# A second weight left whole in float32 for batch 0, with a new table of order, in a three-stage attention and mixture kernel on one core

## The chip, the core and the metric

The kernel runs on one core of one Trainium2 chip. The core has a matrix engine (PE in the profile; its weight loads are the row PEld), a vector engine (DVE), a scalar engine (ACT), a general engine (POOL) and a queue that issues transfers (SP). The metric is the device time of one execution in microseconds (us), lower is better.

## The reference

Three stages follow one another on a batch of 4 sequences of 576 tokens with 512 features.

```python
# 1 windowed attention, 8 heads of 64: four plain (window 32), four dilated by 4
attn = softmax(where(mask, q @ k.T / 8, -1e9)) @ v
# 2 gated mixture
xk = mu_k * x + (1 - mu_k) * x_prev ; xr = mu_r * x + (1 - mu_r) * x_prev
k  = relu(xk @ w_k) ; v = (k * k) @ w_v ; r = sigmoid(xr @ w_r)
x  = r * v
# 3 gated unit with a spatial product
u, v = split(relu(x @ w_in)) ; v_n = normalise(v)
out  = (u * (w_spatial @ v_n + b_spatial)) @ w_out
```

w_k and w_in are 512x1024, w_v is 1024x512, w_r and w_out are 512x512. All inputs arrive as 64-bit words; one 128x512 piece of a weight is 512 KB on its way in.

## The kernel before

**Precision.** A float32 product is made of three reduced-precision products (float32r): both operands are split into a high and a low part (`halves` for activations, `split` for weights), and high·high, high·low and low·high are summed. In the trace such a product is a triple, for the weight w_r `xh,wr`, `xl,wr`, `xh,wr`. A weight named in `WHOLE` is treated otherwise in batch 0: `product` is called with `whole_`, and one real float32 matmul (two records in the trace) takes the unsplit number and the unsplit activation. Such a weight is split only after batch 0, by `split_whole`, before batch 1 needs it. Before, only "wk" stands in `WHOLE`.

**A weight's way in.** `split_weight` cuts a weight into 128x512 chunks (8 of wk, 4 of wr, 8 of wv). For each, SP loads 512 KB of words into one of four half rooms (the tiles `room`, numbers 81 and 82). ACT takes the high word into a number tile and scales the low word in place, DVE joins the two with a SCALAR_TENSOR_TENSOR that reads `room`; I call it the joining. Only then is the half room free for the load four chunks later. The number tile is one of four `temps`, or, for a whole weight, a tile of its own (`wk_..._2`). Without `WHOLE` the split follows: a CAST for the high part (ACT or DVE), a subtraction for the low part (POOL or DVE).

**Batch 0.** Its tokens are computed in two parts, 256 and 320 wide; later batches in two halves of 288. wv's split chunks lie where batch 0's attention inputs (`early`) were, so they are written after the last reader of `early`. The product with wv needs all eight chunks of wv: an output of 128x256 is 24 matmuls, three for each chunk.

**Order.** A planner (`Plan`) holds every step with a cost for each engine that may do it, a priority, and its dependencies. It simulates the engines and from that fixes the order of instructions on each engine and, where two or three engines may do a step, which does it. `TUNE` shifts the priorities and the choice of engine. In gaps that it foresees on PE in the first 100 us the planner puts matmuls on constants (`const-bfloat16-1.0`) that compute nothing; I call them fillers. `keep_warm` in `att` puts more of them between the scores of batch 0. The Tile framework adds waits and buffers, so the fixed order is what the chip executes.

**Names.** `nat_turn` turns batch 0's q and k with PE transposes, `together` puts scores of both head groups into one step. `psM`, `psS`, `psT`, `psB` are PSUM banks, `kr` and `sq_dt.float32r` hold relu and square, `ld` and `vw` are loads of later q, k and v. Nearly every instruction is recorded at one line of a helper (L499 before, L500 after).

Of the kernel before, what the change touches and what calls it, by code (L numbers as in the profile page):

```python
# [37 lines left out]
def blocks(dil):  # L38
# [14 lines left out]
WHOLE = ("wk",)  # L53
# [24 lines left out]
    ('nat', 0, 0): {'nat': (-822, -93004, 792, 22)},  # L78
    ('nat', 0, 1): {'nat': (8004, -315342, 792, 22)},
    ('nat', 1, 0): {'nat': (82855, -4474, 792, 22)},  # L80
    ('nat', 1, 1): {'nat': (-35255, 93970, 792, 22)},
    ('nat', 2, 0): {'nat': (-40032, -157092, 792, 22)},
    ('out', 0): {'egh': (25273, -268581, 0, -800), 'egl': (43089, -174119, 792, 0), 'psB': (-4330, 117521, 792, 22), 'ot': (-59436, 43359, -200, 800), 'out': (49470, 139244, 792, 22)},
    ('out', 1): {'egh': (-167582, 160854, 0, 2000), 'egl': (53746, 288389, 1500, 800), 'psB': (-134988, -179435, 792, 22), 'ot': (-56627, 219801, -200, -300), 'out': (16484, -315151, 792, 22)},
    ('out', 2): {'egh': (17548, -207273, 200, 22), 'egl': (107706, 139205, 792, 300), 'psB': (-159311, 193150, 792, 22), 'ot': (-28034, -383613, -600, -300), 'out': (-205845, -31242, 792, 22)},
    ('out', 3): {'egh': (-158193, -49852, 200, 2000), 'egl': (-111996, -51605, 400, -800), 'psB': (115712, 235954, 792, 22), 'ot': (11988, -24299, 200, 22), 'out': (15709, 251770, 792, 22)},
# [18 lines left out]
    ('sc', 0, 1, 1): {'psM': (-28310, -110097, 792, 22), 'psS': (-63150, -50215, 792, 22)},  # L105
# [17 lines left out]
    ('start',): {'ident': (-6484, -23532, 792, 22), 'identb': (-15068, 269113, 792, 22), 'xok': (48253, 184201, 792, 22), 'mask': (807, 217415, 400, 2000)},  # L123
# [387 lines left out]
def kernel(  # L511
# [61 lines left out]
    ident = get("cp", [P, P], F32, "ident")  # L573
# [1468 lines left out]
```

## Time and profile before

| | |
|---|---|
| Median of 3 runs | 577.19 us (576.16 to 577.32) |
| The profiled execution | 578.83 us, its span 577.1 us |
| Busy: PE, PEld, DVE, ACT, POOL | 97%, 87%, 61%, 44%, 16% of the span |
| Granted TensorE clock | 1.00 in the profiled execution, in nearly every stretch of 10 us |

The span runs from the first to the last instruction; the profiled execution's own time has some 1.7 us around it. Fillers count as busy time of PE, so 97% says less than it seems for the first 84 us.

### The profile page before, as it was taken

Reading aid. Unit: us, or ns where it says so; the run is one execution under the profiler, and the core shown is the slowest. Engines: PE = TensorE matmul, PEld = TensorE weight load, DVE = VectorE, ACT = ScalarE, POOL = GpSimd, SP = SyncE. Lnnn points to the kernel's source line nnn. Section 1 sums busy time; section 2 is a strip of 40 time slices with the busy share of each in tenths; the row PEclk is TensorE's granted clock in tenths of the full one; section 3 lists DMA queues with packets and bytes.
Section 4 is the critical chain, followed back from the end, with each engine's and each line's share of the span. In section 5 each row is a group of like instructions: output and inputs, shape, how many; then the busy total and the mean of one; then the engine's idle time right before and its main releaser. Section 6 shows DMA issues by size and latency. Waiting matters only on the chain.

```text
span 577.1 us, 13816 instructions
## 1 busy us (share of the span) xinstructions
PE 558.9 (97%) x5800; PEld 503.8 (87%) x5813; DVE 354.2 (61%) x784; ACT 252.7 (44%) x579; POOL 92.5 (16%) x115
## 2 busy tenths in 40 slices
PE   8889889999999999999999999999999999999997
PEld 4557677899899999999999999989889989998996
DVE  1699876987988785444975332489456337733540
ACT  1689845423545633713877242386113114311412
POOL 1111023300633402111001010013301210000040
PEclk9999999999999999999999999999999999999999
DMA  9958985356552150311340010231010020001002
GB/s 185 260 160 257 210 133 89 64 102 123 93 89 38 56 123 1 94 37 37 109 132 22 1 26 0 64 104 36 19 37 0 20 92 0 1 1 73 1 1 91
DMA packets 96253, 43.08 MB, mean 75 GB/s; under 512 B 81536, under 2 KB 89216, under 8 KB 96192
## 3 DMA queue, kind: packets, MB, share of 16 engines
q1 hardware_dynamic: 96192, 42.21, 31.4%
q8 instruction: 45, 0.74, 0.5%
q14 instruction: 16, 0.13, 0.1%
HBM read 37.47 MB, written 4.72 MB: 73 GB/s over the span
## 4 chain that ended last, share of the span: by engine, by line
PE 79%; DVE 10%; DMA 5%; ACT 3%; issue 2%; SPq 1%; DVEq 0%; ACTq 0%
PE psM L499 56%; PE psB L499 16%; PE psT L499 4%; DMA room<-in_moe_w_v_dram 3%; PE psS L499 2%; DVE xm L499 1%; DVE st L499 1%; DVE pr L499 1%; DMA room<-in_moe_w_r_dram 1%; DVE kr L499 1%; DMA early<-in_k_dram 1%; DVE wk L499 1%; DMA ld<-in_k_dram 1%; DVE xh L499 1%; SPq L499 1%
## 5 line engine op out<-in xcount | busy, mean ns | idle before, releaser
L499 PE MATMUL psM<-xh,wk 128*128 128x288 f32 (+2 forms) x512 | 124.2, 329 | 2.5 <-DVE xh L499 1.1
L499 PE MATMUL psM<-sq_dt.float32r,wv 128*128 128x288 f32 (+2 forms) x768 | 113.4, 298 | 2.3 <-ACT x L499 1.3
L499 PEld LDWEIGHTS psM<-sq_dt.float32r,wv 128*128 128x128 f32 x768 | 104.8, 188 | 5.0 <-ACT x L499 2.7
L499 PEld LDWEIGHTS psM<-xh,wk 128*128 128x128 f32 x512 | 87.6, 188 | 11.4 <-DVE xh L499 2.2
L499 PE MATMUL psM<-xh,wr 128*128 128x288 f32 (+2 forms) x256 | 63.0, 306 | 2.3 <-ACT xh L499 0.9
L499 PE MATMUL psM<-xl,wk 128*128 128x288 f32 x192 | 56.5, 294 | 0.0
L499 PE MATMUL psM<-x2h,wi 128*128 128x288 f32 x256 | 56.1, 297 | 0.0
L499 ACT ACTIVATE kr<-psM 128x288 f32<-128x288 f32 (+2 forms) x51 | 21.0, 411 | 67.8 <-PE psM L499 64.5
L499 PEld LDWEIGHTS psM<-xh,wr 128*128 128x128 f32 x256 | 44.4, 188 | 4.3 <-ACT xh L499 1.1
L499 POOL TENSOR_TENSOR xl<-xm,xh 128x288 fp32r<-128x288 f32 (+1 forms) x30 | 26.6, 896 | 130.4 <-ACT xh L499 74.9
L499 PEld LDWEIGHTS psM<-x2h,wi 128*128 128x128 f32 x256 | 42.7, 188 | 1.2 <-ACT u L499 0.7
L499 PE MATMUL psB<-wi,x2h 128*128 128x512 f32 x128 | 40.3, 396 | 0.0
L499 PE MATMUL psB<-wo,gh 128*128 128x512 f32 (+1 forms) x136 | 40.2, 379 | 0.0
L499 PE MATMUL psM<-x2l,wi 128*128 128x288 f32 x128 | 37.9, 296 | 0.9 <-DVE x2l L499 0.9
L499 PE MATMUL psM<-wsh,vl 128*128 128x288 f32 x128 | 37.9, 296 | 0.2 <-DVE vl L499 0.2
L499 PE MATMUL psM<-xl,wr 128*128 128x288 f32 (+2 forms) x128 | 37.9, 296 | 0.2
L499 PE MATMUL psM<-wsh,vh 128*128 128x288 f32 x128 | 37.9, 296 | 0.0
L499 PE MATMUL psM<-wsl,vh 128*128 128x288 f32 x128 | 37.7, 294 | 0.0
L499 PEld LDWEIGHTS psM<-xl,wk 128*128 128x128 f32 x192 | 36.1, 188 | 0.0
L499 DVE SCALAR_TENSOR_TENSOR xm<-x,mu,xm 128x288 f32<-128x288 f32 (+2 forms) x56 | 31.3, 564 | 5.8 <-ACT xm L499 5.4
L499 DVE SCALAR_TENSOR_TENSOR x<-x,psM 128x288 f32<-128x288 f32 (+2 forms) x32 | 14.4, 453 | 32.8 <-PE psM L499 25.7
L499 DVE TENSOR_TENSOR g<-psM,bb 128x288 f32<-128x288 f32 x32 | 14.3, 453 | 31.2 <-PE psM L499 27.8
(161 smaller groups left out, 1097.1 us busy)
## 6 DMA issues: line engine op xcount, KB each, us to landing
vw<-in_v_dram SPq DMA_DIRECT2D x36, 128.0 KB, 3.1
room<-in_moe_w_k_dram SPq DMA_DIRECT2D x8, 512.0 KB, 7.4
room<-in_moe_w_v_dram SPq DMA_DIRECT2D x8, 512.0 KB, 6.3
raw<-in_moe_w_in_dram SPq DMA_DIRECT2D x8, 512.0 KB, 3.8
ld<-in_q_dram SPq DMA_DIRECT2D x48, 72.0 KB, 2.6
ld<-in_k_dram SPq DMA_DIRECT2D x48, 72.0 KB, 2.7
vw<-in_v_dram SPq DMA_DIRECT2D x8, 288.0 KB, 5.6
room<-in_moe_w_r_dram SPq DMA_DIRECT2D x4, 512.0 KB, 4.8
```

What stands on the lines that cost most here:

```text
L499: return self.tc.keep_in_program_order(getattr(self.engine, name)(*args, **kw))
```

## The change

"wr" joins `WHOLE`; batch 0 multiplies w_r as one float32 matmul per term and does not split the activations for it; w_r is split after batch 0. The costs by which the planner places `nat_turn` and `together` change, and all entries of `TUNE` are new, found for the mean of replays with disturbed durations. Two of its lines stand for the table.

```diff
-WHOLE = ("wk",)
+WHOLE = ("wk", "wr")
...
-    ('w', 'wr'): {'tmp': (-19737, -299053, 792, 22), 'low': (-26769, 116870, 792, 22), 'part0': (-18161, 187096, 200, 300), 'part1': (-37782, 29061, -200, -300)},
+    ('w', 'wr'): {'whole': (-146522, -222248, 792, 22), 'low': (247288, 121722, 792, 22)},
...
+    ('w2', 'wr'): {'part0': (51813, 179976, -200, -800), 'part1': (185010, 430438, 1500, -300)},
...
-            cost, ins = 0.43 * w, 4 * len(its)
+            cost, ins = 0.94 * w, 4 * len(its)
...
-            cost, ins = len(its) * (30 + 0.4 * n), 2 * len(its)
+            cost, ins = len(its) * (70 + 0.41 * n), 2 * len(its)
...
+        steps = max(x[2] for x in infos)
...
-            for i in range(max(x[2] for x in infos)):
+            for i in range(steps):
...
-            {"pe": max(x[2] for x in infos) * (157 if b else 200 + 40 * len(infos)) + 150 * (b > 0) + sum(x[5] for x in infos)}, emit,
+            {"pe": steps * (157 if b else 94 + 63 * len(infos)) + (150 if b else 320 * -(-steps // 3)) + sum(x[5] for x in infos)}, emit,
```

Three places show how the order moves. On PE, at the start of batch 0's first product with w_r (256 wide), stood before, with `wr_0_0` a high and `wr_0_1` a low part:

```order
L499 MATMUL psM_100<-xh_0_579,wr_0_0_753 128x256
L499 MATMUL psM_100<-xl_585,wr_0_0_753 128x256
L499 MATMUL psM_100<-xh_0_579,wr_0_1_760 128x256
L499 LDWEIGHTS const-bfloat16-1.0
L499 MATMUL psT_119<-const-bfloat16-1.0 128x512
L499 MATMUL psM_100<-xh_0_582,wr_0_0_793 128x256
L499 MATMUL psM_100<-xl_587,wr_0_0_793 128x256
L499 MATMUL psM_100<-xh_0_582,wr_0_1_802 128x256
```

and after the change, `wr_0_2` being the whole number:

```order
L500 MATMUL psM_100<-xh_0_426,wr_0_2_677 128x256
L500 LDWEIGHTS const-bfloat16-1.0
L500 MATMUL psT_119<-const-bfloat16-1.0 128x512
L500 MATMUL psM_100<-xh_0_484,wr_0_2_692 128x256
L500 MATMUL psM_100<-xh_0_424,wr_0_2_726 128x256
L500 MATMUL psM_100<-xh_0_486,wr_0_2_762 128x256
```

Three matmuls became one at 32 places (16 of them 256 wide, 16 of them 320 wide). In the whole program the fillers go from 83 to 68.

On DVE, from the joining of wr's second chunk to that of its third, stood before:

```order
L499 SCALAR_TENSOR_TENSOR temps<-temps,room_82 128x512
L499 CAST sq_dt.float32r<-kr_746 128x256
L499 CAST wr_0_0_793<-temps 128x512
L499 TENSOR_TENSOR sq_dt.float32r<-kr_746,sq_dt.float32r 128x256
L499 SCALAR_TENSOR_TENSOR temps<-temps,room_81 128x512
```

and after:

```order
L500 SCALAR_TENSOR_TENSOR wr_0_2_692<-wr_0_2_692,room_82 128x512
L500 TENSOR_SCALAR st_105<-st_105 128x6
L500 RECIPROCAL st_105<-st_105 128x6
L500 CAST wr_0_0_731<-wr_0_2_692 128x512
L500 TENSOR_TENSOR pr_104<-pr_104,st_105 128x384
L500 TENSOR_TENSOR sq_dt.float32r<-kr_628,sq_dt.float32r 128x256
L500 SCALAR_TENSOR_TENSOR wr_0_2_726<-wr_0_2_726,room_81 128x512
```

The early casts of wr stay on DVE; wr's four subtractions, which stood here on DVE and POOL, are on POOL and behind the last subtraction of wk. Softmax steps of batch 0's last attention chunk (`pr_104`) moved down to this place.

On SP, around the loads of wv's last four chunks, stood before:

```order
L499 DMA vw_90<-in_v_dram 64x18x64
L499 DMA vw_90<-in_v_dram 64x8x64 x2
L499 DMA room_81<-in_moe_w_v_dram 128x1024
L499 DMA vw_90<-in_v_dram 64x2x64
L499 DMA room_82<-in_moe_w_v_dram 128x1024
L499 DMA ld_109<-in_q_dram 32x18x32 x3
L499 DMA room_81<-in_moe_w_v_dram 128x1024
L499 DMA ld_109<-in_q_dram 32x18x32
L499 DMA ld_110<-in_k_dram 32x18x32
L499 DMA room_82<-in_moe_w_v_dram 128x1024
```

and after:

```order
L500 DMA vw_89<-in_v_dram 64x2x64
L500 DMA vw_89<-in_v_dram 64x8x64
L500 DMA room_81<-in_moe_w_v_dram 128x1024
L500 DMA vw_89<-in_v_dram 64x8x64
L500 DMA room_82<-in_moe_w_v_dram 128x1024
L500 DMA ld_109<-in_q_dram 32x18x32 x2
L500 DMA room_81<-in_moe_w_v_dram 128x1024
L500 DMA ld_109<-in_q_dram 32x18x32 x2
L500 DMA ld_110<-in_k_dram 32x18x32
L500 DMA room_82<-in_moe_w_v_dram 128x1024
L500 DMA ld_110<-in_k_dram 32x18x32 x3
L500 DMA vw_89<-in_v_dram 64x18x64
```

The largest load of v (64x18x64, 288 KB) moved from ahead of wv's fifth chunk to behind its eighth.

## Rows read from the trace of the kernel before

**Rows 1.** Busy time by stretch; columns: stretch, length, engines, clock, DMA share, GB/s.
```profile
0.00:84.00 84.00, 72.69 (x941) 51.80 (x955) 61.50 (x141) 55.57 (x117) 12.36 (x24) 1.00 0.92 204
84.00:577.00 493.00, 486.19 (x4861) 451.99 (x4860) 292.73 (x644) 197.09 (x462) 80.11 (x91) 1.00 0.22 53
57.00:84.00 27.00, 23.21 (x149) 18.84 (x150) 22.65 (x43) 18.89 (x40) 3.96 (x7) 1.00 1.02 175
84.00:130.00 46.00, 45.95 (x629) 38.70 (x631) 35.42 (x70) 17.62 (x39) 11.11 (x11) 1.00 0.50 86
```

**Rows 2.** PE's waits from 84 us on: engine, tile, releaser, total, times, longest.
```profile
PE psM L499 <- DVE x2l L499: 0.9, 1, 0.9
...
PE psT L499 <- DVE pr L499: 0.2, 1, 0.2
```

**Rows 3.** Chain that ended last, near 69 and 83 us: start, length, what.
```profile
69.35 9.07 DMA room<-in_moe_w_v_dram
...
83.36 17.49 PE psM L499 x81
```

**Rows 4.** PE in order of time: start, length, matmul, out, in, count.
```profile
57.84 2.56 PE L499 MATMUL psT<-const-bfloat16-1.0 128*128 128x512 bf16 x11
60.30 0.70 PE L499 MATMUL psM<-xh,wk 128*128 128x256 f32 x2
...
83.36 1.10 PE L499 MATMUL psM<-sq_dt.float32r,wv 128*128 128x256 f32 x7 [0.92 <-DVE wv L499]
...
88.85 12.01 PE L499 MATMUL psM<-xh,wk 128*128 128x320 f32 x44
100.69 0.33 PE L499 MATMUL psS<-mask,identb 128*128 128x384 bf16 x1
...
111.56 0.46 PE L499 MATMUL psM<-xh,wr 128*128 128x320 f32 x2
...
112.00 0.46 PE L499 MATMUL psM<-xh,wr 128*128 128x320 f32 x2
```

**Rows 5.** DVE in order of time, from wr's first joining to wv's last subtraction.
```profile
47.92 0.69 DVE L499 SCALAR_TENSOR_TENSOR temps<-temps,room 128x512 uint32<-128x512 uint32 x1 [0.17 <-ACT temps L499]
48.53 0.29 DVE L499 CAST sq_dt.float32r<-kr 128x256 fp32r<-128x256 f32 x1
48.73 0.42 DVE L499 CAST wr<-temps 128x512 fp32r<-128x512 f32 x1
49.07 0.42 DVE L499 TENSOR_TENSOR sq_dt.float32r<-kr,sq_dt.float32r 128x256 fp32r<-128x256 f32 x1
49.40 0.69 DVE L499 TENSOR_TENSOR wr<-temps,wr 128x512 fp32r<-128x512 f32 x1
50.01 0.70 DVE L499 SCALAR_TENSOR_TENSOR temps<-temps,room 128x512 uint32<-128x512 uint32 x1
...
51.56 1.71 DVE L499 SCALAR_TENSOR_TENSOR temps<-temps,room 128x512 uint32<-128x512 uint32 x1
...
54.15 1.76 DVE L499 SCALAR_TENSOR_TENSOR temps<-temps,room 128x512 uint32<-128x512 uint32 x1
...
56.87 0.68 DVE L499 SCALAR_TENSOR_TENSOR temps<-temps,room 128x512 uint32<-128x512 uint32 x1
...
79.69 0.69 DVE L499 SCALAR_TENSOR_TENSOR temps<-temps,room 128x512 uint32<-128x512 uint32 x1 [0.43 <-ACT temps L499]
...
81.97 0.76 DVE L499 STREAM_TRANSPOSE kT<-ld 128x576 f32<-128x576 f32 x1
82.67 0.64 DVE L499 TENSOR_TENSOR wv<-temps,wv 128x512 fp32r<-128x512 f32 x1
```

**Rows 6.** POOL's 128x512 subtractions in order of time.
```profile
51.33 1.39 POOL L499 TENSOR_TENSOR wr<-temps,wr 128x512 fp32r<-128x512 f32 x1 [20.36 <-DVE wr L499]
54.00 1.36 POOL L499 TENSOR_TENSOR wr<-temps,wr 128x512 fp32r<-128x512 f32 x1 [1.28 <-ACT wr L499]
...
111.09 1.61 POOL L499 TENSOR_TENSOR wk<-wk,wk 128x512 fp32r<-128x512 f32 x1
```

More of the change, by code (lines that the diff above doesn't have):

```diff
@@ L49, in blocks @@
     ]
-WHOLE = ("wk",)
+WHOLE = ("wk", "wr")
 TUNE = {
[20 rows of a table removed]
[L78 to L86, printed above, removed]
[18 rows of a table removed]
-    ('sc', 0, 1, 1): {'psM': (-28310, -110097, 792, 22), 'psS': (-63150, -50215, 792, 22)},
[17 rows of a table removed]
-    ('start',): {'ident': (-6484, -23532, 792, 22), 'identb': (-15068, 269113, 792, 22), 'xok': (48253, 184201, 792, 22), 'mask': (807, 217415, 400, 2000)},
[12 rows of a table removed]
-    ('val', 0, 0, 0): {'psT': (-34158, -48716, 792, 22), 'x': (-52668, -255147, 200, 0)},
-    ('val', 0, 0, 1): {'psT': (76565, 66919, 792, 22), 'x': (287811, -108015, -600, 800)},
-    ('val', 0, 1, 0): {'psT': (-76048, -191051, 792, 22), 'x': (105794, 405919, -200, 0)},
-    ('val', 0, 1, 1): {'psT': (1224, -26729, 792, 22), 'x': (-122606, 27116, 200, -300)},
-    ('val', 1, 0): {'psT': (10503, 218319, 792, 22), 'x': (32870, 1272, -600, 2000)},
-    ('val', 1, 1): {'psT': (-107452, 91347, 792, 22), 'x': (26648, 147373, 400, -800)},
-    ('val', 2, 0): {'psT': (45455, 30237, 792, 22), 'x': (-51975, 173400, 0, 800)},
-    ('val', 2, 1): {'psT': (323, -27166, 792, 22), 'x': (176049, 403471, 0, -800)},
-    ('val', 3, 0): {'psT': (16562, -271025, 792, 22), 'x': (31029, 51724, 1500, 0)},
-    ('val', 3, 1): {'psT': (65210, 140835, 792, 22), 'x': (-17857, -365445, 0, -800)},
[26 rows of a table removed]
-    ('ws',): {'raw2': (-11211, 145195, 792, 22), 'wst': (-68893, -60709, 792, 22), 'psB': (-57368, 20150, 792, 22), 'wsh': (80040, 47783, -200, -300), 'wsl': (12028, 551114, 792, 22), 'wslz': (-87801, -207339, 792, 22), 'bb': (70427, -230127, 792, 22)},
[5 rows of a table removed]
[20 rows of a table added]
+    ('nat', 0, 0): {'nat': (-216361, 63261, 792, 22)},
+    ('nat', 0, 1): {'nat': (-122479, -39726, 792, 22)},
+    ('nat', 1, 0): {'nat': (-53641, -255652, 792, 22)},
+    ('nat', 1, 1): {'nat': (74163, -7809, 792, 22)},
+    ('nat', 2, 0): {'nat': (46058, -347879, 792, 22)},
+    ('out', 0): {'egh': (129179, -268581, -600, 800), 'egl': (-181388, -174119, 400, 800), 'psB': (32171, 90959, 792, 22), 'ot': (-298828, -72354, 200, -800), 'out': (-178157, 297879, 792, 22)},
+    ('out', 1): {'egh': (107723, 160854, -200, -300), 'egl': (-186104, 288389, 0, 0), 'psB': (-150019, 104024, 792, 22), 'ot': (18863, 546702, 1500, -300), 'out': (-77504, -391091, 792, 22)},
+    ('out', 2): {'egh': (146366, -207273, -600, 2000), 'egl': (78348, 139205, -600, -300), 'psB': (-8720, 225495, 792, 22), 'ot': (-171072, -166882, 400, 800), 'out': (300769, -59453, 792, 22)},
+    ('out', 3): {'egh': (-259613, -49852, 400, -800), 'egl': (218830, -51605, 0, 300), 'psB': (256969, 633757, 792, 22), 'ot': (-116737, 169061, 792, 0), 'out': (-106705, 197271, 792, 22)},
[18 rows of a table added]
+    ('sc', 0, 1, 1): {'psM': (48543, -110097, 792, 22), 'psS': (-62657, -50215, 792, 22)},
[17 rows of a table added]
+    ('start',): {'ident': (36562, -23532, 792, 22), 'identb': (-225224, 269113, 792, 22), 'xok': (-95250, 241899, 792, 22), 'mask': (-131520, 217415, 400, 2000)},
[12 rows of a table added]
+    ('val', 0, 0, 0): {'psT': (-129193, -10067, 792, 22), 'x': (89734, -280738, 200, 2000)},
+    ('val', 0, 0, 1): {'psT': (77074, 10438, 792, 22), 'x': (95205, 146882, 792, 800)},
+    ('val', 0, 1, 0): {'psT': (154860, -91697, 792, 22), 'x': (114696, 367535, -200, 2000)},
+    ('val', 0, 1, 1): {'psT': (-28123, 54316, 792, 22), 'x': (13797, -368486, 200, -300)},
+    ('val', 1, 0): {'psT': (-126639, 467794, 792, 22), 'x': (-142952, -124387, 792, 300)},
+    ('val', 1, 1): {'psT': (357327, 248792, 792, 22), 'x': (5562, 383455, 400, 22)},
+    ('val', 2, 0): {'psT': (238499, 628795, 792, 22), 'x': (-188714, 18329, -600, -300)},
+    ('val', 2, 1): {'psT': (-181640, -218926, 792, 22), 'x': (62789, 50969, -600, 2000)},
+    ('val', 3, 0): {'psT': (-88318, -305454, 792, 22), 'x': (-155592, 71474, 0, 0)},
+    ('val', 3, 1): {'psT': (-147886, -18842, 792, 22), 'x': (240808, -90005, 400, -300)},
[27 rows of a table added]
+    ('ws',): {'raw2': (-148230, 110027, 792, 22), 'wst': (113261, -28656, 792, 22), 'psB': (11675, -194170, 792, 22), 'wsh': (30789, -133680, 200, 300), 'wsl': (-474, 938038, 792, 22), 'wslz': (51562, -207339, 792, 22), 'bb': (987, -230127, 792, 22)},
[5 rows of a table added]
```

194 rows, old and new, of the table TUNE are left out of this document.

## The prediction

> **What bounds the kernel now.** I read the busy time by stretch first, then PE's waits, then the chain that ended last, and then the engines in order of time around the place where that chain changes engine.
>
> The busy time by stretch cuts the program in two [rows 1]. From 84 us to the end PE is busy for 486.19 of 493 us; of the rest some 3.6 us is the tail behind the last matmul, and what remains is seven single waits, the longest 0.9 us and the shortest 0.2 us [rows 2]. Over that length time goes only with the number and width of matmuls. Before 84 us PE is idle for 84 − 72.69 = 11.3 us, and much of its busy time is fillers: eleven of them take 60.30 − 57.84 = 2.46 us, 0.224 us each [rows 4], so the 83 fillers of the order are some 18.6 us that compute nothing.
>
> The chain says what ends the first part [rows 3]: the load of wv's eighth chunk from 69.35 us, 9.07 us long, then some steps on ACT and DVE, and at 83.36 us PE takes over for good. PE itself waited 0.92 us there for the low part of wv [rows 4]. I call 83.36 us the gate. Every 256-wide output of the product with wv needs that chunk, so behind the gate lies the rest of this product, all of batch 0's second part and batches 1 to 3. The order of the changed kernel has the same there: all of wr's and wk's 256-wide products ahead of it, and the 32 products `xh,wk` 128x320 behind it or in its shadow. So the new time is the old one, plus how far the gate moves, plus how much PE work behind it grows, plus any change of the waits behind it.
>
> What sets the gate is a pair. In 57 to 84 us the transfer engines are busy for a share of 1.02, at 175 GB/s, DVE for 22.65 of 27 us and PE for 23.21 with its fillers [rows 1]. Loads of wv are issued when a joining on DVE frees a half room, and then share the transfer engines with small-packet loads of q, k and v.
>
> **The change, part by part.** The sum is made against the profiled execution, 578.83 us (its span is 577.1), which lies 1.64 us above the median; I take the same difference off the median.
>
> *The whole float32 product, behind the gate.* 44 records, 22 products of 128x320 in float32, take 100.69 − 88.85 = 11.84 us, 0.538 us each; a triple of the same width takes 112.00 − 111.56 = 0.44 us [rows 4]. 16 products of this width become dearer by 0.098 us: +1.6 us, all on PE's path.
>
> *The same, ahead of the gate.* Scaled with the width 256/320 a product costs 0.08 us more, 16 of them 1.25 us. PE has 11.3 us of idle time and 18.6 us of fillers there, so I cost this at nothing; with that cover gone it is +1.25 us. Fifteen fillers fewer (3.4 us of busy time) are worth nothing either, since they lie in waits.
>
> *Splits that leave the start.* Before, from wr's first joining (47.92 us) to wv's first (56.87) DVE needs 8.95 us [rows 5]. Two of the joinings in it take 1.71 and 1.76 us instead of 0.69 and begin while POOL subtracts at 51.33 for 1.39 us and at 54.00 for 1.36 us [rows 6]: 2.1 us of standing still. After, no POOL subtraction stands in this stretch. By starts in [rows 5] a joining takes 0.61 us, a 512-wide cast 0.34, a 256-wide cast 0.20, a 256-wide subtraction 0.33. The stretch now holds four joinings (2.44), four 512-wide casts (1.36), two 256-wide casts (0.40), four 256-wide operations of two more kinds priced as the subtraction (1.32), one scaling (0.3), two 384-wide softmax steps between 0.33 and 0.61 (0.94) and two tiny ones (0.3): 7.0 us, 2.0 less. It is no more than that because softmax steps of the last attention chunk moved in. Loads of wv start up to 2.0 us earlier; the lower bound is nothing, because the transfer engines are full from 57 us on.
>
> *The large load of v.* 288 KB moved from ahead of wv's fifth chunk to behind its eighth. At 175 GB/s [rows 1] that is 1.7 us of transfer ahead of the gate, from nothing (if the queue had a pause there) to 1.7. Its reader is batch 1's attention, whose first scores come at 100.69 us [rows 4] and its values later, so it has over 15 us of room.
>
> *The end of the chain.* From the eighth joining at 79.69 to the start of the last subtraction at 82.67 go 3.0 us, in which DVE also mixes two activations for w_r and transposes kT (81.97) [rows 5]. After, DVE has one subtraction (0.61) and that transpose (0.70) between them, behind a joining of 0.61: 1.9 us, so −1.1, or nothing if kT's load comes late and stands in front of it.
>
> *What moved behind the gate.* wr's four low parts, and seven of wk's that were on DVE, are subtracted on POOL between the gate and batch 1's products. POOL is busy for 11.11 of the 46 us from 84 to 130 [rows 1]; twelve of 1.39 to 1.61 us [rows 6] are 18 us. Eight square subtractions go to DVE in return. That is free as long as DVE keeps up; it has 46 − 35.42 = 10.6 us idle there.
>
> A rule of the Trainium skill speaks against this part: "SBUF — State Buffer", section "Who interferes with whom", says that a GpSimd instruction reading SBUF and a DVE instruction with two SBUF inputs exclude each other for the whole instruction. The row of 51.56 us bears it out. By that rule up to twelve DVE instructions would each stand still for as long as a POOL subtraction runs, some 18 us in all by the durations above, more than the idle time; the trace's own price is in the first rival.
>
> *New priorities everywhere.* Behind the gate they can win at most the seven waits, or lose; I take no change, with −1.5 to +2 us as bounds (half of the 3.2 us that are idle without the tail, and two waits like the longest).
>
> *Sum.* The gate could move by 2.0 + 1.7 + 1.1 = 4.8 us at most. The first two overlap where the transfer engines are the limit, so I take half of the first: 1.0 + 1.7 + 1.1 = 3.8. With +1.6 this is −2.2 us: 576.6 against 578.83, and **575.0 us** for the median.
>
> **Rivals.**
>
> *POOL's twelve subtractions hold DVE up (slower).* Each overlap cost DVE 1.0 us before (1.71 against 0.69). Eleven more are 11 us against 10.6 idle, less 3.2 us for the eight square subtractions now on DVE, plus 4.3 us for seven of wk's now gone from it: 11.7 us of room. It just suffices; it decides as soon as a third of that room lies at the wrong moment, since batch 1's first terms with wk then wait for a low part. Some 4 us of waits give 577.19 − 2.2 + 4 = 579.0 us. Against it: instructions that read one SBUF operand or PSUM need not wait, and most softmax steps are such.
>
> *The gate stays (slower).* The last attention chunk's softmax and values moved down, and wv's split chunks go where their inputs lay; if those readers end late, the splits of wv do too and the gate with them. Then only +1.6 us is left: 578.8.
>
> *The gate moves by as much as PE grows (no change).* Transfers full from 57 us on would leave 1.7 of the 3.8 us: 577.1.
>
> *All of it adds up (faster by more).* 4.8 earlier, 1.6 more work, 1.5 of waits gone: 572.5.
>
> **How the numbers follow.** The forecast (573.6 to 576.3) has 0.45, the larger gain 0.15, no change 0.18, POOL 0.13, the gate that stays 0.09. A measurement of this kernel tells 0.2% (1.15 us) from no change. Faster are the larger gain and nearly all of the forecast, 0.57; within 0.2% are the third case and the forecast's edge, 0.21; slower are the two others, 0.22. The range from 572.0 to 578.9 leaves out the outer half of the larger gain and the worst of POOL's case, under 2 in 10.
>
> **What would show it.** Right: wv's eighth chunk lands before 76 us, the last wait of PE for wv ends near 79.5 us, no joining between wr's and wv's first is longer than 0.75 us, 22 products 128x320 with wr or wk at 0.54 us each, and the stretch behind the gate as full as before. Wrong: a gate at 83 us or later; waits of PE for `wk` or `wr` near batch 1's first products; DVE operations of 1.6 us beside POOL's subtractions in 85 to 130 us; or new single waits over 1 us in the later batches, where I saw no reason for any.

## The result: faster, by more than twice what was forecast

The changed kernel takes 569.72 us (median of four executions, 567.52 to 578.05) against 576.97 us (576.16 to 577.32) for the kernel before: a ratio of 0.9864 [0.9827, 0.99]. The ratio leaves out the execution at 578.05 us, whose granted clock was lower (0.988). Timed twice more beside the kernel before, the ratio was 0.9907 [0.9877, 0.9936] and 0.9915 [0.9883, 0.9948], so a typical gain is 5 to 8 us. Forecast were 575.0 us and a range from 572.0 to 578.9.

The profiled execution took 567.52 us, its span 565.7. Its busy time by stretch, in the columns of [rows 1]:

```profile
0.00:84.00 84.00, 78.73 (x964) 58.63 (x976) 62.83 (x147) 54.04 (x114) 4.66 (x16) 1.00 0.95 214
84.00:565.70 481.70, 474.87 (x4793) 442.60 (x4791) 281.50 (x636) 203.00 (x461) 83.71 (x90) 1.00 0.21 52
84.00:130.00 46.00, 45.42 (x726) 37.12 (x725) 34.05 (x61) 20.71 (x48) 18.15 (x16) 1.00 0.48 92
```

The span is 11.4 us shorter, nearly all of it ahead of the gate. The chain that ended last, where [rows 3] had the load of wv's eighth chunk at 69.35 and PE at 83.36:

```profile
61.41 7.84 DMA room<-in_moe_w_v_dram
...
70.58 0.54 DVE temps L500
...
71.22 0.67 DVE wv L500
71.93 3.14 PE psM L500 x21
```

It is the same chain, 7.9 us earlier at the load and 11.4 us at PE. PE's wait at 83.36 was for the last low part of wv; the one at 71.93 is for the low part before it. DVE in order of time, as [rows 5], from the joinings of wr's four chunks to wv's first, and at wv's eighth:

```profile
44.20 0.69 DVE L500 SCALAR_TENSOR_TENSOR wr<-wr,room 128x512 uint32<-128x512 uint32 x1
...
45.99 0.69 DVE L500 SCALAR_TENSOR_TENSOR wr<-wr,room 128x512 uint32<-128x512 uint32 x1
...
48.01 0.69 DVE L500 SCALAR_TENSOR_TENSOR wr<-wr,room 128x512 uint32<-128x512 uint32 x1
...
50.02 0.69 DVE L500 SCALAR_TENSOR_TENSOR wr<-wr,room 128x512 uint32<-128x512 uint32 x1
...
51.43 0.69 DVE L500 SCALAR_TENSOR_TENSOR temps<-temps,room 128x512 uint32<-128x512 uint32 x1
...
70.58 0.69 DVE L500 SCALAR_TENSOR_TENSOR temps<-temps,room 128x512 uint32<-128x512 uint32 x1 [1.18 <-ACT room L500]
...
71.79 0.77 DVE L500 STREAM_TRANSPOSE kT<-ld 128x576 f32<-128x576 f32 x1
72.49 0.65 DVE L500 TENSOR_TENSOR wv<-temps,wv 128x512 fp32r<-128x512 f32 x1
```

No joining stands still any more, wr's first to wv's first take 7.23 us instead of 8.95, and the last low part of wv begins at 72.49 instead of 82.67. Below, this start is the gate, and "behind" is the time from it to the end of PE's last matmul (562.51 here, 573.51 before).

PE from the gate on, where [rows 4] had 83.36 and the triples:

```profile
71.93 2.54 PE L500 MATMUL psM<-sq_dt.float32r,wv 128*128 128x256 f32 x19 [0.32 <-DVE wv L500]
74.31 3.46 PE L500 MATMUL psM<-xh,wk 128*128 128x320 f32 x12
...
91.23 0.70 PE L500 MATMUL psM<-xh,wr 128*128 128x320 f32 x2
91.77 0.70 PE L500 MATMUL psM<-xh,wk 128*128 128x320 f32 x2
...
94.43 0.81 PE L500 MATMUL psM<-xh,wr 128*128 128x320 f32 x2
95.07 1.78 PE L500 MATMUL psM<-xh,wk 128*128 128x320 f32 x6
```

A whole product of 128x320 takes 91.77 − 91.23 = 0.54 us, as costed, and 0.64 behind scores. PE's waits from 84 us on, against the seven of [rows 2]:

```profile
PE psM L500 <- DVE x2l L500: 0.9, 1, 0.9
PE psM L500 <- DVE x L500: 0.7, 1, 0.7
PE psM L500 <- ACT xh L500: 0.7, 1, 0.7
PE psT L500 <- DMA vw<-in_v_dram: 0.6, 1, 0.6
PE psM L500 <- DVE xh L500: 0.6, 1, 0.6
```

They add up to 3.5 us, the seven before to 2.9. None is for wk or wr.

**The pair exaggerates.** Second profiles were taken of both kernels. The kernel before then had its gate at 79.30 and 492.3 us behind, the changed one at 74.43 and 489.8. So the gate moved by 10.2 us in one pair and 4.9 in the other, and behind it 0.8 and 2.6 us were won. A third profile of the changed kernel (after_third) has its gate at 79.51. In the second profile of the kernel before no joining from wr's first to wv's first stands still (0.68 to 0.69 us each), and the stretch takes 8.02 us: the two long joinings of [rows 5] are not in every execution.

### The profile page after: what moved, and what is told of

Same layout as the page of the kernel before. It is cut to its first block, busy times and chain, and to the rows that moved or that the text cites. A ratio compares the mean times of both kernels' runs of the same rounds, so it can differ in the third digit from the quotient of the medians.

```text
span 565.7 us, 13681 instructions
## 1 busy us (share of the span) xinstructions
PE 553.6 (98%) x5755; PEld 501.2 (89%) x5766; DVE 344.3 (61%) x782; ACT 257.0 (45%) x575; POOL 88.4 (16%) x105
## 4 chain that ended last, share of the span: by engine, by line
PE 87%; DVE 3%; DMA 3%; ACT 2%; SPq 2%; issue 1%; DVEq 0%; ACTq 0%
PE psM L500 60%; PE psB L500 18%; PE psT L500 6%; SPq L500 2%; PE psS L500 2%; DMA room<-in_moe_w_v_dram 1%; DMA vw<-in_v_dram 1%; DVE xm L500 1%; DMA ld<-in_k_dram 1%; DVE xl L500 1%; ACT xh L500 0%; DVE xh L500 0%; ACT room L500 0%; ACT xm L500 0%; ACT wv L500 0%
## 5 line engine op out<-in xcount | busy, mean ns | idle before, releaser
L500 PE MATMUL psM<-xh,wk 128*128 128x288 f32 (+2 forms) x512 | 119.1, 326 | 1.5 <-DVE x L500 0.7
L500 PE MATMUL psM<-x2h,wi 128*128 128x288 f32 x256 | 54.8, 296 | 0.0
L500 DVE TENSOR_TENSOR sq_dt.float32r<-kr,sq_dt.float32r 128x288 fp32r<-128x288 f32 (+2 forms) x54 | 26.8, 502 | 26.3 <-ACT sq_dt.float32r L500 25.8
L500 POOL TENSOR_TENSOR xl<-xm,xh 128x288 fp32r<-128x288 f32 x18 | 15.6, 876 | 127.6 <-ACT xh L500 67.8
L500 DVE BATCH_NORM_STATS2 bn<-vt 128x6 f32<-128x512 f32 x18 | 12.4, 691 | 37.6 <-ACT vt L500 37.5
```

The costliest lines, as they stand in the source:

```text
L500: return self.tc.keep_in_program_order(getattr(self.engine, name)(*args, **kw))
```

## The experiments

In most, the order of all engines was written out as one list, and only entries of that list or their engines were edited. "Start" is the list up to the last low part of wv, "rest" what follows. Ratios are to the kernel before in the same comparison.

| Run | Median us | Ratio | Gate us | Behind us |
|---|---|---|---|---|
| after_again | 570.47 | 0.9907 [0.9877, 0.9936] | 74.43 | 489.8 |
| after_third | 569.98 | 0.9915 [0.9883, 0.9948] | 79.51 | 491.4 |
| before_again | 576.15 | 0.9998 [0.9979, 1.0017] | 79.30 | 492.3 |
| float_old_order | 580.51 | 1.0075 [1.0048, 1.0103] | 78.83 | 494.7 |
| start_new_rest_old | 576.41 | 1.0003 [0.9977, 1.003] | 73.56 | 494.3 |
| start_old_rest_new | 575.31 | 0.9983 [0.9964, 1.0002] | 82.56 | 490.1 |
| table_old_ops | 573.91 | 0.9957 [0.9934, 0.9981] | 78.34 | 489.4 |
| old_ops_rest_new | 575.0 | 0.9956 [0.9937, 0.9974] | 82.24 | 489.7 |
| v_ahead | 573.25 | 0.9937 [0.9913, 0.9961] | 78.76 | 490.4 |
| loads_behind | 569.32 | 0.9887 [0.986, 0.9915] | 75.52 | 492.1 |
| casts_late | 570.94 | 0.9911 [0.9878, 0.9945] | 74.26 | 489.8 |
| casts_act | 571.15 | 0.9938 [0.9915, 0.9961] | 75.78 | 490.0 |
| pool_more | 572.01 | 0.9922 [0.9892, 0.9951] | 77.43 | 490.0 |
| tiny_fillers | 571.37 | 0.992 [0.99, 0.994] | 73.24 | 491.7 |
| no_late_fillers | 571.38 | 0.9908 [0.9873, 0.9943] | 78.77 | 491.2 |
| half_loads | 571.56 | 0.99 [0.9879, 0.9921] | 76.49 | 490.3 |
| half_products | 571.16 | 0.9909 [0.9882, 0.9936] | 76.38 | 489.8 |
| half_products_light | 571.93 | 0.9925 [0.99, 0.995] | 77.08 | 490.0 |

The two columns on the right come from one profile each, often of another execution than the median, and the gate scatters between executions of one kernel, by up to 7 us (72.49 to 79.51 in the changed one). The behind scatters by 1.5.

**Both kernels again.** Unedited; after_third ran beside loads_behind.

> The changed kernel once more, unaltered. The pair of profiles differs by 11.3 us, the timed runs by 7.9. If the time behind the gate is a matter of scatter, this profile stands near 569 us and its last low part of wv again starts near 72.5 us, 10 us ahead of before; if the extra 3 us behind the gate are real, the time from the first float32 product 128x320 to PE's last matmul is again near 488.2 us (before: 489.2).

> The changed kernel unaltered, on the chip of the three runs beside it, as what they are compared with. Its two profiles so far have the last low part of wv start at 72.5 and 74.4 us and 488.2 and 488.0 us from the first float32 product 128x320 to PE's last matmul; this one again lies between 72 and 75 us and within 0.5 us of 488.1.

> The kernel before, unaltered, for a second profile of it. One profile alone says how long it takes from the first float32 product 128x320 to PE's last matmul (489.2 us), against 487.9 to 488.6 in five of the new order behind the gate. If the 1.6 us by which the new order with the old instructions (487.6) is shorter are real, this one is again within 0.5 us of 489.2; its gate (last low part of wv) lies at 79 to 83 us.

The gain is smaller than first timed, and the gate depends on the execution (last section). Two expectations failed: after_third's gate is not in 72 to 75 us, and before_again takes 490.7 us and not 489.2 from the first product 128x320 (80.94) to PE's last matmul (571.63).

**The parts apart.** float_old_order is the product alone, every instruction where the kernel before had it:

```diff
-WHOLE = ("wk",)
+WHOLE = ("wk", "wr")
```

The mixed lists join the two orders at the gate (shown in short: `seq_` stands for a written-out list); table_old_ops and old_ops_rest_new keep the triples:

```diff
-seq = seq_after
+seq = seq_after[:gate] + seq_before[gate:]
...
+seq = seq_before[:gate] + seq_after[gate:]
```

> The float32 product of w_r alone: every instruction that both kernels have stands in the order and on the engine that it had before; the splits that leave batch 0 are gone, wr's four low parts follow wk's on POOL, and four mixings of x that need a free tile wait for it. Theory A (the new order of the start gave most of the gain): the chain of loads up to wr's first joining stays where it was (47.9 us), the stretch from wr's to wv's first joining shrinks from 8.95 to about 7 us, the gate comes 2 to 5 us earlier, and the time falls by 2 to 4 us to 573 to 575. Theory B (the work that leaves the start gave it, in whatever order): the gate comes 8 to 10 us earlier and the time is 568 to 570. My prediction's price of the product (+1.6 us behind the gate): PE's time from the first product 128x320 to the end grows by 1.6 us; by the changed kernel's records it grows by no more than 0.3.

> Both parts of the change up to the last low part of wv, and the old order behind it. Theory A and theory B alike put the gate where the changed kernel has it (72.5 us). If the new order behind the gate is worth nothing, as I took it, the time is that of the changed kernel within 1 us (568 to 570); if it is worth the 2.6 us by which the records behind the gate differ from my sum, the time is 571 to 572.

> The float32 product with the old order up to the last low part of wv, and the new order behind it. Theory A: within 1 us of the float32 product alone in the old order (573 to 575). If the new order behind the gate is worth 2 to 3 us: 570.5 to 573. Theory B: as the changed kernel, 568 to 570.

> The new order alone: the instructions of before (w_r as triples, split in batch 0), each where the changed kernel has it; wr's low parts follow their casts, the splits of x follow its mixing. If the two parts add up, the order is worth the 10.0 us between the float32 product in the old order (580.5) and both (570.5), and this kernel stands near 567. If the new order needs the room that the float32 product makes on DVE in the start, the gate falls back by 2 to 5 us and the time is 570 to 574. If order is nothing without the float32 product: 576 to 577.

> The instructions of before in their old order up to the last low part of wv, and in the new order behind it. The new order with the old instructions took 2.5 us off. If 1.6 us of that lie behind the gate, as PE's records say, this kernel takes 487.3 to 488.0 us from the first float32 product 128x320 to PE's last matmul and is 1 to 2.5 us faster than before; if the order's gain lies in the start, it is within 0.7 us of before.

Of some 576.5 us: the float32 product alone makes the kernel slower, by 0.0075 × 576.5 = 4.3 us; the order alone makes it faster by 2.5 (table_old_ops), and its rest alone by 2.5 too (old_ops_rest_new), so without the product the new start is worth nothing that can be told. With the product, the new start is worth 4.2 (float_old_order to start_new_rest_old) and the new rest 5.3 (to start_old_rest_new); together they make the 9.7 us from float_old_order to after_again. The product costs 4.3 us in the old order and brings 2.4 to 2.9 in the new one (table_old_ops to the two later timings of the changed kernel, whose intervals just overlap with it). So product and order can't be priced apart. Both theories of float_old_order were wrong, and the two mixed lists came out slower than every theory for them had it. What makes the product pay in the new order alone is not shown. Behind the gate the product in the old order costs 3 us and not 1.6; PE's waits there from 84 us on show two that the kernel before had not at this place (its `DVE pr` of 0.2 us came at 151 us, this one at 110.7):

```profile
PE psM L499 <- ACT kr L499: 1.0, 1, 1.0
...
PE psT L499 <- DVE pr L499: 0.8, 1, 0.8
```

**The large load of v.** v_ahead puts it back; loads_behind takes eight loads of batch 1's q, k and v out of wv's way, and two of its transposes, with four later loads, behind the gate.

```diff
 DMA vw_89<-in_v_dram 64x8x64
+DMA vw_89<-in_v_dram 64x18x64
 DMA room_81<-in_moe_w_v_dram 128x1024
...
 DMA ld_110<-in_k_dram 32x18x32 x3
-DMA vw_89<-in_v_dram 64x18x64
```

> The changed kernel with the 288 KB load of v back ahead of wv's fifth chunk. My term: 1.7 us of transfer go back ahead of the gate, so wv's eighth chunk lands 1.7 us later, the last low part of wv starts near 74 to 76 us instead of 72.5 to 74.4, and the time grows by 1 to 2 us against the changed kernel (ratio to before .992 to .994 instead of .989). Rival: the load fills a pause of the queue, nothing moves by more than 0.5 us.

> The changed kernel with the eight remaining loads of batch 1's v, q and k that stand among wv's loads moved behind wv's eighth, and the two transposes of them on DVE moved behind the last low part of wv. Theory: from 51 us on the loads of wv share the transfer engines with them (288 KB of v cost 2.0 us between wv's fourth and fifth joining in v_ahead), so 288 KB of v and 360 KB of q and k less bring wv's eighth joining 2 to 4 us earlier, to 67 to 69 us, and the time falls by 2 to 3 us against the changed kernel. Rival: the loads fill pauses that the turn of the half rooms leaves; the joining moves by less than 1 us. A third outcome: batch 1's first scores wait for q and k, and PE loses behind the gate what it won.

The joinings of wv's fourth and fifth chunk in v_ahead:

```profile
61.60 0.69 DVE L500 SCALAR_TENSOR_TENSOR temps<-temps,room 128x512 uint32<-128x512 uint32 x1 [0.91 <-ACT room L500]
...
68.95 0.68 DVE L500 SCALAR_TENSOR_TENSOR temps<-temps,room 128x512 uint32<-128x512 uint32 x1
```

They are 7.35 us apart, and 5.31 in two profiles of the changed kernel (56.95 to 62.26, 59.21 to 64.52): the load stood 2.0 us in the way, 1.7 were costed. By the two later ratios the load costs 0.2 to 0.3% of the time, 1.3 to 1.7 us, though the intervals overlap. This prices the load in the changed order: in the kernel before, with the load at that place, the same two joinings are 5.5 us apart in both profiles. With eight more loads behind wv's last, the fifth to the eighth joining take 6.5 us instead of 8.0 to 9.7, but some 2 us come back behind the gate (492.1 against 490.0, with a scatter of 1.5), a wait of PE of 0.6 us for kT among them, whose transpose now stands there. The time is the lowest of all; beside it the changed kernel took 569.98, and the intervals overlap.

**What sets the pace of wr's and wv's splits.** Each takes load off one engine: casts_late moves ten 512-wide casts of wk and wr from DVE to behind the gate; casts_act moves six steps from ACT to DVE on top; half_loads, on top of that, loads half of each chunk of wr and of wv's first four; half_products halves batch 0's first 32 products with wk, half_products_light does so on top of casts_act.

```diff
-CAST wk_0_0_506<-wk_0_2_482 128x512
...
-ACTIVATE kr_624<-kr_624 128x256
+TENSOR_TENSOR kr_624<-kr_624 128x256
...
-nc.sync.dma_start(raw_of(kr), s[:, r, 2 * c0 : 2 * (c0 + CH)])
+nc.sync.dma_start(raw_of(kr)[:, :n], s[:, r, 2 * c0 : 2 * c0 + n])
...
-nc.tensor.matmul(ps[:, :cols], l, r, start=j == 0, stop=j == n - 1)
+nc.tensor.matmul(ps[:, :m], l, r[:, :m], start=j == 0, stop=j == n - 1)
```

> The changed kernel with ten 512-wide casts of wk and wr (high parts that nobody reads before batch 1) moved on DVE from ahead of the last low part of wv to behind it. Theory: between 35 and 60 us DVE sets the pace of the loads (busy 4.8 to 5.0 of each 5 us), so ten casts of 0.34 us bring wv's first joining up to 3.4 us and the gate 2 to 3.4 us earlier: 566.5 to 568.5. Rival: the transfers set the pace (share 0.82 to 1.2), the gate stays within 1 us, 569 to 571. A third outcome: the low parts on POOL come too late for batch 1's first product with w_k, and PE waits for wk near 122 us.

> The kernel with ten casts moved behind the gate, and six operations of batch 0 (four squares, a cast and a copy of 0.42 to 0.48 us) given from ACT to DVE, between wk's fifth and wv's fourth joining. Moving the casts alone left the joinings where they were, so DVE is not the pace there; ACT was busy for 4.8 to 4.9 of each 5 us. If ACT is the pace, 2.5 us less of it bring wv's fourth joining (56.95 us, 57.15 with the casts moved) 1.5 to 2.5 us earlier and the time 1 to 2 us lower. If the turn of a half room is (load 4.5 us, two steps on ACT, joining, about 7.2 us for four chunks), the joinings keep their 1.8 us and the fourth stays within 0.5 us.

> The kernel with ten casts moved and six operations given from ACT to DVE, and with only the first half of each chunk of wr and of wv's first four chunks loaded (256 KB instead of 512; the other half of the half room keeps what was there, so the numbers of these chunks are not the reference's). With all loads whole, relieving DVE and then ACT left the pace of the joinings at 1.86 us a chunk. If the transfer sets it (512 KB at about 290 GB/s are 1.8 us), the seven steps from wk's eighth to wv's third joining shrink from 13.0 to 9 to 11 us. If something else sets it, they stay within 0.7 us of 13.0.

> The changed kernel with batch 0's first 32 float32 products with w_k computed for 128 of their 256 tokens (the rest of the bank keeps what was there, so the output is not the reference's). In the changed kernel's chain PE holds nearly every piece from 36 to 51 us, and the joinings wait for results of these products on DVE and ACT. If PE sets the pace, the seven steps from wk's eighth to wv's third joining (13.0 us) shrink to 10 to 12 us, less than the 3.5 us that the products save only because ACT and DVE are full too. If the pace is ACT's and DVE's own work, they stay within 0.5 us of 13.0.

> The same shorter products in the kernel that has ten casts moved and six operations given from ACT to DVE (output not the reference's). Lightening DVE, then ACT, then the loads left the seven steps at 13.0 to 13.1 us each time. If PE sets the pace, they now fall to 9.5 to 11 us; if a fifth thing does, they stay near 13.

From the joining of wk's eighth chunk to that of wv's third, seven steps, the changed kernel takes 55.30 − 42.29 = 13.0 us. casts_act and half_loads, from DVE in order of time:

```profile
45.61 0.68 DVE L500 SCALAR_TENSOR_TENSOR wk<-wk,room 128x512 uint32<-128x512 uint32 x1
...
58.68 0.69 DVE L500 SCALAR_TENSOR_TENSOR temps<-temps,room 128x512 uint32<-128x512 uint32 x1
```

```profile
47.81 0.68 DVE L500 SCALAR_TENSOR_TENSOR wk<-wk,room 128x512 uint32<-128x512 uint32 x1
...
60.88 0.69 DVE L500 SCALAR_TENSOR_TENSOR temps<-temps,room 128x512 uint32<-128x512 uint32 x1
```

13.07 us in both, 12.96 in casts_late, 12.71 and 12.85 with the halved products. So none of DVE, ACT, PE and the transfers sets this pace alone, by the work that was taken off it, and none of the five is faster than the changed kernel clear of the noise. What does set it stays open.

**POOL beside DVE.** pool_more repeats the only subtraction of a low part that the changed kernel has on POOL ahead of the gate, four times more.

```diff
 TENSOR_TENSOR wk_0_1_365<-wk_0_2_303,wk_0_0_351 128x512
+TENSOR_TENSOR wk_0_1_365<-wk_0_2_303,wk_0_0_351 128x512 x4
```

> The changed kernel with four further POOL subtractions (wk's first low part computed again) among the four joinings of wr, where before had such subtractions. If each holds a joining for 1.0 us, as the two did before, joinings of 1.7 us appear, the stretch from wr's to wv's first joining grows from 7.2 to 9 to 11 us and the time by 2 to 4 us against the changed kernel. If DVE has other work beside them that does not wait, the stretch grows by less than 1 us.

The four were meant to stand among wr's joinings. POOL had nothing to wait for and ran all five at once, from 21.66 to 28.95 us, beside wk's splits. POOL, and DVE beside it, in order of time:

```profile
21.66 7.29 POOL L500 TENSOR_TENSOR wk<-wk,wk 128x512 fp32r<-128x512 f32 x5 [0.49 <-DVE wk L500]
```

```profile
22.06 0.69 DVE L500 TENSOR_REDUCE st<-pr 128x8 f32<-128x512 f32 x1
22.67 0.55 DVE L500 TENSOR_TENSOR pr<-psS,st 128x384 f32<-128x384 f32 x1
23.25 1.57 DVE L500 COPY vw<-vw 32x1024 f32<-32x1024 f32 x1
...
26.13 1.70 DVE L500 SCALAR_TENSOR_TENSOR wk<-wk,room 128x512 uint32<-128x512 uint32 x1
27.76 1.75 DVE L500 TENSOR_TENSOR pr<-pr,st 128x512 f32<-128x512 f32 x1
```

A joining takes 1.70 us instead of 0.69, and a copy 1.57 instead of the 0.68 that it takes in the changed kernel, while a product out of PSUM (0.55) and a reduction (0.69) keep their time. PE then waits 2.32 us for POOL (from 26.65 to 28.97). Neither the gate (77.43) nor the ratio is outside the scatter of the changed kernel, so the price in the end time isn't settled by this run.

**The fillers.** tiny_fillers replaces six of the first twelve by 64 matmuls of 8 columns, so that PE has 116 instructions more and hardly other work; no_late_fillers leaves out the eleven behind wk's fifth joining.

```diff
 MATMUL psM_91<-xh_0_424,wk_512_2_613 128x256
-LDWEIGHTS const-bfloat16-1.0
-MATMUL psT_119<-const-bfloat16-1.0 128x512
 MATMUL psM_91<-xh_0_486,wk_512_2_625 128x256
```

> The changed kernel with six of the first twelve fillers replaced by 64 matmuls of 8 columns, 116 PE instructions more. PE stands still for 1.0 to 2.3 us at its 956th recorded instruction in every profile of the new order of the start, in the middle of a pass over values, and at the 701st in every one of the old order, 255 earlier, with nothing else to wait for; a stretch at the lower clock follows in most of them. If this is the fetch of the next block of 256 instructions through the same full transfer engines, the stop comes again at the 956th instruction, which is now 116 earlier in the program (among products and scores near 29 us), or goes, and not in the pass over values. If it belongs to that pass, it stays there, at the 1072nd. If the lower clock comes from the stop, its place moves with it.

> The changed kernel without the eleven fillers that stand behind wk's fifth joining. If PE is what the loads wait for from 36 us on, 2.4 us of matmuls that compute nothing are partly on its path: the gate comes 0.5 to 1.5 us earlier and the time falls by as much. If they all lie in waits of PE, nothing moves by more than 0.3 us, and a lower clock in 50 to 70 us may cost 1 to 2 us.

Nothing is won without them: they lie in waits. In no_late_fillers the granted clock is 0.66 in 35 to 45 us and in 60 to 65 us, a mean between the two levels (1.2 and 2.4 GHz).

## Why the prediction came out too small

**The step that failed** is "New priorities everywhere ... I take no change", and with it the +1.6 us behind the gate that stood in the sum alone. Behind the gate the kernel before takes 490.8 and 492.3 us, the changed one 490.0, 489.8 and 491.4: on the mean −1.2 us instead of +1.6 (part of after_third's 491.4 is the lower clock, 0.50 in 80 to 83 us). The forecast was −2.2 us and −5 to −8 came, so 2.8 of the 3 to 6 us between them lie behind the gate, the rest at it. Two things were read wrongly.

First, the triple's price. 0.44 us is that of a triple behind another triple [rows 4]. Most of the 16 follow scores, transposes or products of another kind, and their first matmul takes longer; from the kernel before:

```profile
110.28 0.41 PE L499 MATMUL psM<-xh,wr 128*128 128x320 f32 x1
110.53 0.30 PE L499 MATMUL psM<-xl,wr 128*128 128x320 f32 x1
110.68 0.31 PE L499 MATMUL psM<-xh,wr 128*128 128x320 f32 x1
110.83 0.38 PE L499 MATMUL psT<-ident,pr 128*128 128x128 f32 x2
```

This one takes 110.83 − 110.28 = 0.55 us. Added up from start to start of PE's records, the 16 triples took 8.28 us (0.517 each), the 16 whole products 8.50 (0.531): +0.2, not +1.6. In float_old_order they took 10.00, with the wait for `pr` among them.

Second, "PE is busy for 486.19 of 493 us" was taken for full, and the waits view for all that an order could win. PE's records say otherwise. I add up, from start to start and less the waits that the view lists, the matmuls of batches 1 to 3 that carry w_k, w_r, w_v and the values:

| us | `sq_dt,wv` 128x288 (576) | `xh,wk` (384) | `xh,wr` (192) | `pt,vw` (912) | Sum |
|---|---|---|---|---|---|
| before | 77.81 | 54.93 | 26.50 | 14.88 | 174.1 |
| before_again | 77.87 | 54.90 | 26.50 | 14.88 | 174.1 |
| after | 77.22 | 53.13 | 26.37 | 15.05 | 171.8 |
| after_again | 77.24 | 53.11 | 26.34 | 15.05 | 171.7 |

The third profile of the changed kernel has 171.7, table_old_ops, with the new order and the triples, 171.9, float_old_order 173.9. So the order wins 2.4 us that no wait row lists. In the first pair, batch 0's 96 matmuls `sq_dt,wv` 128x320 give 0.8 of it back (14.9 to 15.6), the float32 products 0.2 and the listed waits 0.6, which leaves the 0.8 us that were won behind the gate.

Nearly all of it is short waits. Among the matmuls of the three weights in this table that have another 128-wide one before and behind them, 0.13 us is usual. In the two profiles of the kernel before, 23 and 25 take over 0.16 us because the next one starts 0.02 to 0.05 us after DVE or ACT released it, or because they stand right behind such a place; in each of the three of the changed kernel only 4 do. They lie 3.1 and 3.3 us above the usual before and 0.9 after, which is 2.2 to 2.4 of the 2.5 us that these three kinds won. One such place, from the kernel before, on PE and DVE:

```profile
150.07 0.42 DVE L499 TENSOR_SCALAR kr<-psM 128x288 f32<-128x288 f32 x1
150.11 0.83 PE L499 MATMUL psM<-xh,wk 128*128 128x288 f32 x2
150.78 0.30 PE L499 MATMUL psM<-xl,wk 128*128 128x288 f32 x1
```

The two take 150.78 − 150.11 = 0.67 us instead of 0.27; the second starts at 150.54, 0.05 us after DVE has read a PSUM bank out (150.07 + 0.42 = 150.49). The 4 or 5 long ones without a release are as many in both kernels.

**Point by point.**

- *The gate.* Costed were 3.8 us. The pairs show 10.2 and 4.9; from the times, a gain of 5 to 8 us less the 1.2 behind leaves 4 to 7. Cut at wr's first, wv's first and wv's eighth joining, the pairs are 3.7 + 1.7 + 3.7 + 1.1 and 1.3 + 0.8 + 1.7 + 1.1, against 0 + 1.0 + 1.7 + 1.1 in the sum. So the second pair bears out the three terms; for the piece ahead of wr's first joining the sum had none. That joining, at 47.92 and 47.75 us before, comes at 44.20, 46.44 and 48.69 in the changed kernel, which is too wide to price the piece. The "all of it adds up" rival, 572.5 us, was the nearest.
- *Splits that leave the start.* 7.0 us forecast, 7.23 to 7.25 measured; before it was 8.95 and 8.02, so 0.8 to 1.7 was won. That DVE's sum sets this stretch is wrong: with ten casts fewer, four of them in this stretch (casts_late), it is still 7.23. So the 7.0 us were met by luck.
- *Ahead of the gate* the whole product was taken as free. No row of the changed kernel shows a price for it; in the old order 4.3 − 3 leaves at most some 1.3 us.
- *The large load of v* was worth 2.0 us in the changed order (1.7 forecast). Its room held: PE's only wait for a load of v, 0.6 us, which the kernel before hadn't, comes at 180 us, and the values of batch 1 that need this load begin at 112.77 without one.
- *The end of the chain* took 72.49 − 70.58 = 1.91 us, 1.9 forecast.
- *POOL's twelve subtractions* were nearly free. Eleven stand behind the gate and take 14.6 us (18 were costed), one ahead of it at 21.23. POOL, DVE and PE at two places:

```profile
96.99 1.27 POOL L500 TENSOR_TENSOR wk<-wk,wk 128x512 fp32r<-128x512 f32 x1 [4.17 <-PE psM L500]
97.48 1.13 DVE L500 SCALAR_TENSOR_TENSOR xh<-x,mu,xh 128x320 f32<-128x320 f32 x1 [0.48 <-ACT xh L500]
98.67 1.34 PE L500 MATMUL psM<-xh,wr 128*128 128x320 f32 x4 [0.56 <-DVE xh L500]
...
112.25 5.66 POOL L500 TENSOR_TENSOR wr<-wr,wr 128x512 fp32r<-128x512 f32 x4
113.80 1.62 DVE L500 TENSOR_TENSOR pr<-pr,st 128x384 f32<-128x384 f32 x1
```

DVE is held at both (0.55 us is usual for either instruction), but has 46 − 34.05 = 12.0 us of idle time in 84 to 130 us. The waits for wk or wr that the rival foresaw don't come; the hold at 97.48 costs PE 0.56 us all the same, through the activation `xh` and not through a low part, and 0.57 in both later profiles. pool_more shows that the price per overlap, about 1 us, was right, and which instructions pay it; that agrees with the Trainium skill, "SBUF — State Buffer", section "Who interferes with whom", by which a reduction never contends and a two-input instruction does. The rival's "instructions that read one SBUF operand ... need not wait" doesn't hold throughout: the copy in pool_more has one input and took 1.57 us instead of 0.68.
- *The markers*: wv's eighth chunk landed at 69.25 us (before 76), PE's last wait for wv ended at 71.93 (79.5 was forecast).

## What to carry to other kernels

A cheaper operation and the order around it are one change: here the same product is 4.3 us dearer in the old order and over 2 us cheaper in one arranged for it, so neither half tells what the whole does. Price a product from the sum over all its places, from start to start, and not from the tidiest row; and a matrix engine that is 98.6% busy may still hide over 2 us of short waits, which its records show from start to start. Where the start of a kernel scatters between executions, take two profiles of each before sizing a term from one.

## What the runs showed of the hardware

**PE stops where nothing is awaited.** In the changed kernel, in the middle of a row of value products, and in tiny_fillers:

```profile
32.07 0.65 PE L500 MATMUL psT<-pt,early 64*64 64x32 f32 x26
33.88 0.31 PE L500 MATMUL psT<-pt,early 64*64 64x32 f32 x6 [1.17 <-issue]
```

```profile
31.49 0.24 PE L500 MATMUL psS<-turned 64*32 64x64 f32 x1
33.19 0.54 PE L500 MATMUL psS<-turned 64*32 64x64 f32 x23 [1.46 <-issue]
```

The stop falls at the 956th to 962nd of PE's records (matmuls, weight loads and some ten of its sequencer) in all profiles with the new start but pool_more, and at the 701st to 706th in those with the old one: some 255 apart. tiny_fillers has 116 more instructions ahead of it, so its stop is at another place of the program but at the 962nd record. It took 0.7 to 2.8 us. The profile's page of the changed kernel has a queue for instructions, 0.74 MB in 45 packets, 16.4 KB each:

```profile
q8 instruction: 45, 0.74, 0.6%
```

This agrees with the Trainium skill, "Runtime: NRT & Kernel Launch", section "Instruction fetch mechanics": instructions come in blocks of 16 KiB, 256 each, over a transfer queue of the engine's own. The trace bears it out: 11558 records of PE are 257 for each of the 45 packets. In all 19 profiles that have the stop PE goes on 2.4 to 2.9 us after one of these packets began, while the stop itself begins anywhere from 0.15 us before the packet to 1.9 us after it. In pool_more, where PE came late to this record, the packet had begun over 5 us earlier and there is no stop. So the stop is a wait for that packet. The Trainium skill calls the crossing mostly hidden; here it isn't, and the transfer engines are full at that moment (share 0.98 in 30 to 34 us). That the full engines delay the packet is argued from this, not shown.

**The lower clock follows the longer pauses.** after_again, where the stop took 1.56 us, by stretch:

```profile
33.00:35.00 2.00, 0.44 (x16) 0.30 (x9) 1.16 (x3) 0.19 (x1) 0.00 (x0) 1.00 0.96 381
35.00:37.00 2.00, 1.67 (x32) 0.88 (x28) 1.45 (x4) 1.31 (x3) 0.00 (x0) 0.50 0.81 287
```

PE is busy for 0.44 of 2 us, and the next stretch has 0.50, the level of 1.2 GHz. After stops of 1.01 (casts_late) and 1.17 us (the changed kernel) the clock stayed at 1.00, after one of 1.15 us in float_old_order it fell to 0.57 in 30 to 34 us. In pool_more the wait of 2.32 us for POOL did the same: 0.50 in 30 to 34 us. Of after_third's six executions two had a mean clock of 1.000, at 568.89 and 569.55 us; the profiled one, with a stop of 1.92 us, had 0.991 and took 575.89. Behind 84 us the clock is 1.00 in every profile, so this bears on the start alone. In the changed kernel the gate goes with it (72.49 at a mean clock of 1.000, 74.43 at 0.997, 79.51 at 0.991); in the kernel before it doesn't (82.67 at 1.000, 79.30 at 0.997), and what moves its gate stays open.
